# Attention with 16 queries per head: one late store in place of fifteen

## The chip, the cores and the metric

The kernel runs on one core of one Trainium2 chip. Its time is the device time of that core in microseconds (us). The core has a matrix engine (TensorE, PE in the profile), a vector engine (VectorE, DVE), an activation engine (ScalarE, ACT), GpSimd (POOL) and SyncE (SP), which here does nothing but issue transfers. All of them run their own instruction streams and meet at semaphores. Transfers between HBM and SBUF are carried out by 16 DMA engines. SyncE and ScalarE each have a queue to them; in the profile SyncE's is q1 and ScalarE's q10.

## The reference, cut to what matters

```
B, H, Sq, Skv, Dh = 8, 16, 16, 2048, 256        # all bfloat16
scores = einsum('bhqd,bhkd->bhqk', q, k) * Dh ** -0.5
attn   = softmax(scores, axis=-1)
out    = einsum('bhqk,bhkd->bhqd', attn, v)
```

There are 128 heads. K and V are 134 MB each and are read once; q and the output are 1 MB each.

## The kernel before, in words

**Blocks.** Eight heads make a block of 128 rows of output (8 heads by 16 queries); there are G = 16 blocks, numbered 0 to 15, and `last` is 15. A block needs 8 MB of K, which comes as two halves of 4 MB, and 8 MB of V. The 128 rows are the partitions of the result.

**Buffers.** `SL` has four slots of 4 MB in SBUF: VA and VB hold one block's V, KA and KB one block's K. Nothing of K or V is held twice, so a slot is loaded again as soon as its readers are done. `O_fin` holds the finished 128 rows of 256 values of one block in bfloat16, 512 bytes in each partition.

**One block.** VectorE transposes the K slots in place (line 196). TensorE multiplies them with the weights made of q into `S_ps` (lines 309 and 310). VectorE takes the maximum, ScalarE makes the exponentials into `P_sb` with their sums (line 292). VectorE transposes those into `PTa` and `PTb`, and ScalarE and VectorE copy them into `PTz` (lines 277, 203 and 205), the weights of the second product. TensorE sums 128 matmuls of V into `O_ps` (line 332). ScalarE evicts `O_ps` with a factor of one over the sum into `O_fin` (`evac`, line 271), and the block is stored.

**The order around the change.** The engines run loops over the blocks, one block apart from one another. In its pass g ScalarE works on the exponentials of block g, makes the first part of the copies, evicts block g - 1, issues its store, and makes the rest of the copies (lines 284 to 302). The eviction waits for the end of block g - 1's matmuls (`c_pv`), for its factor (`c_ri`) and, since there is only one `O_fin`, for the landing of the store before (`s_st`). The store waits for the eviction (`c_ev`). TensorE starts the next block's second product only when `c_ev` says that `O_ps` is empty.

**SyncE's queue.** SyncE issues every load, in this order: q; K of blocks 0 and 1; V of block 0; then in a loop both K halves of block j and V of block j - 1, each behind a wait for the readers of the slot; then K of block 15 in four pieces, V of block 14 in three pieces, and V of block 15 in nine pieces that get smaller (`PIECES`, the last one of two matmuls' rows). Each V piece waits until the matmuls on the rows that it overwrites are done. Behind the last piece SyncE waits for the last eviction, stores block 15 and waits for its landing:

```
eng.wait_ge(c_ev, G + 1)
eng.dma_start(oh[last], O_fin[:]).then_inc(s_fin, 16)
eng.wait_ge(s_fin, 16)
```

GpSimd gives some semaphores their start values, 1 to `c_ev` and 17 to `s_st` among them, so that the first passes find their waits satisfied.

Of the kernel before, what the change touches and what calls it, by code (L numbers as in the profile page):

```python
# [4 lines left out]
ACTF = mybir.ActivationFunctionType  # L5
# [6 lines left out]
BF16 = mybir.dt.bfloat16  # L12
# [8 lines left out]
def bass_standalone__softmax_full_bidir__sampling_kernel(  # L21
# [6 lines left out]
    B, H, SQ, D = q.shape  # L28
# [3 lines left out]
    G = NH // 8  # L32
    last = G - 1
    scale = float(D) ** -0.5
# [3 lines left out]
    ku = k.rearrange("b h s d -> (b h s) d").rearrange("(u p t) d -> u p t d", p=128, t=T)  # L38
    vb = v.rearrange("b h s d -> (b h s) d").rearrange("(g p t) d -> g p t d", p=128, t=2 * T)
    qh = q.rearrange("b h s d -> (b h) (s d)")  # L40
    oh = out.rearrange("b h s d -> (b h s) d").rearrange("(g p) d -> g p d", p=128)

    with ExitStack() as es:
        ec = es.enter_context
# [8 lines left out]

        PTz = ec(nc.sbuf_tensor("PTz", [128, 2, T, 128], BF16))
        mk = ec(nc.sbuf_tensor("mk", [128, 1], F32))
        O_fin = ec(nc.sbuf_tensor("O_fin", [128, D], BF16))
        negm = ec(nc.sbuf_tensor("negm", [128, 1], F32))
        lsum = ec(nc.sbuf_tensor("lsum", [128, 2], F32))
        ltot = ec(nc.sbuf_tensor("ltot", [128, 1], F32))
        rinv = ec(nc.sbuf_tensor("rinv", [128, G + 2], F32))  # L60

        S_ps = ec(nc.psum_tensor("S_ps", [128, 4, 512], F32))
        O_ps = ec(nc.psum_tensor("O_ps", [128, 512], F32))
        X_ps = ec(nc.psum_tensor("X_ps", [128, 512], F32))

        def sem(name):
            return ec(nc.semaphore(name))
# [4 lines left out]
        s_kl = [sem("s_kla"), sem("s_klb")]  # L72
        s_v = sem("s_v")
        s_v0 = sem("s_v0")
        s_st = sem("s_st")
        s_fin = sem("s_fin")
# [9 lines left out]
        c_ri = sem("c_ri")  # L86
        c_cp = sem("c_cp")
# [3 lines left out]
        c_pv = sem("c_pv")  # L91
        c_ev = sem("c_ev")
# [19 lines left out]
        def weights(e, r, x):  # L112
            rows = slice(32 * r, 32 * r + (32 if x else 16))
            m = 32 * r + 16 * x
            if e == x:
                src = PTa[rows, :, 16 * x:16 * x + 16]
            else:
                src = PTb[rows, e:e + T, 16 * x:16 * x + 16]
            return PTz[rows, e, :, m:m + 16], src, mk[rows, :]

        def qx(Q, a):

            return (QTu[32 * a:32 * a + 32, 8 * Q:8 * Q + 8, :, :].rearrange("p u c y -> p c u y"),
                    QXu[32 * Q:32 * Q + 32, a, :, :, :].rearrange("p u c y -> p c u y"))

        def load_k(eng, g, e, slot, t0, n, s):
            eng.dma_start(SL[:, slot, t0:t0 + n, :], ku[2 * g + e, :, t0:t0 + n, :]).then_inc(s, 16)  # L127

        def on_sync(eng):
            def load_v(w, a, n):  # L130

                eng.wait_ge(c_pv, 8 * w + (a + n + C - 1) // C)
                eng.dma_start(VW[:, a:a + n, :], vb[w, :, a:a + n, :]).then_inc(s_p[w][a] if a else s_v, 16)  # L133

            eng.dma_start(QX, qh).then_inc(s_q, 16)  # L135
            for g, s0, s in ((0, VA, s_k0), (1, KA, s_k)):
                for e in range(2):
                    load_k(eng, g, e, s0 + e, 0, T, s[e])

            for e in range(2):  # L140
                eng.wait_ge(c_qk, 4 * e + 4)
                eng.dma_start(VW[:, T * e:T * e + T, :], vb[0, :, T * e:T * e + T, :]).then_inc(s_v0 if e else s_v, 16)
            with nc.Fori(2, last, engines=[SP]) as j:
                for e in range(2):
                    eng.wait_ge(c_qk, 8 * j + 4 * e - 4)
                    load_k(eng, j, e, KA + e, 0, T, s_k[e])
                load_v(j - 1, 0, 2 * T)
            for e in range(2):
                eng.wait_ge(c_qk, 8 * last + 4 * e - 4)
                load_k(eng, last, e, KA + e, 0, T // 2, s_k[e])  # L150
                load_k(eng, last, e, KA + e, T // 2, T // 2, s_kl[e])
            for w in PIECES:
                for a, n in PIECES[w]:
                    load_v(w, a, n)
            eng.wait_ge(c_ev, G + 1)
            eng.dma_start(oh[last], O_fin[:]).then_inc(s_fin, 16)
            eng.wait_ge(s_fin, 16)

        def on_gpsimd(eng):

            for x, n in ([(c_ev, 1), (c_ri, 2), (c_cp, 1), (c_pv, 8), (s_st, 17)] + [(x, 1) for x in s_kl] +
                         [(x, 1) for w in s_p for x in s_p[w].values()]):
                eng.sem_inc(x, n)
            zero = [PTz[:, e].rearrange("p t c -> p (t c)").bitcast(F32) for e in range(2)]
            eng.memset(zero[0], 0.0).then_inc(c_pool, 1)
            eng.wait_ge(c_qt, 2)
            for n in range(12):

                eng.wait_ge(c_cq if n else c_pool, max(n, 1))
                eng.tensor_copy(*qx(1 + n // 4, n % 4)).then_inc(c_cq, 1)  # L170

            eng.wait_ge(c_qt, 6)
            eng.wait_ge(c_qw, 4)
            eng.wait_ge(c_cq, 12)
            eng.memset(zero[1], 0.0).then_inc(c_pool, 1)
# [81 lines left out]
        def on_scalar(eng):  # L257
            def qwb(src):
                for a in range(4):
                    dv = QW[32 * a:32 * a + 32, :, 16 * a:16 * a + 64, :]  # L260
                    dv = bass.AP(tensor=dv.tensor, offset=QW[32 * a:32 * a + 32, 0, 16 * a, :].offset,
                                 ap=[list(dv.ap[0]), [1024 + 512, 2], [2, 64], [1, 2]])
                    eng.activation(dv, src(a), ACTF.Copy, scale=scale).then_inc(c_qw, 1)  # L263

            def evac(n, st):

                eng.wait_ge(c_pv, 8 * n)
                eng.wait_ge(c_ri, 2 * n)

                eng.wait_ge(s_st, st)  # L270
                eng.activation(O_fin[:], O_ps[:, 0:D], ACTF.Copy, scale=rinv[:, bass.ds(n, 1)]).then_inc(c_ev, 1)  # L271

            def copies(e, rs):
                for r in rs:
                    for x in range(2):
                        dst, src, m = weights(e, r, x)
                        eng.activation(dst, src, ACTF.Copy, scale=m if x else 1.0).then_inc(c_cp, 1)  # L277

            eng.wait_ge(c_qt, 2)
            qwb(lambda a: QXu[0:32, a, 0:2, :, :])  # L280
            eng.wait_ge(c_pool, 2)
            eng.wait_ge(c_qt, 6)
            eng.wait_ge(c_mk, 7)
            with nc.Fori(0, G, engines=[ACT]) as g:
                eng.wait_ge(c_qk, 8 * g + 8)
                qwb(lambda a: QTu[32 * a:32 * a + 32, bass.ds(((g + 1) & 15) * 2, 2), :, :])
                eng.wait_ge(c_mx, g + 1)
                for h in range(2):

                    sv = S_ps[:, 2 * h, :]  # L290
                    sv = bass.AP(tensor=sv.tensor, offset=sv.offset, ap=[list(sv.ap[0]), [32, 32], [1, 2], [2, 16]])
                    eng.activation(P_sb[:, 16 + 1024 * h:16 + 1024 * h + 1024], sv, ACTF.Exp,  # L292
                                   bias=negm[:], scale=1.0, accum_out=lsum[:, h:h + 1]).then_inc(c_ex[h], 1)
                eng.wait_ge(c_pt, 4 * g + 4)
                eng.wait_ge(c_pv, 8 * g + 4)
                copies(0, (0, 1))
                gg = eng.to_reg(g)
                with eng.If_ne(gg, 0):
                    evac(g + 1, 16 * g + 1)
                    eng.wait_ge(c_ev, g + 1)  # L300
                    eng.dma_start(oh[(g + 15) & 15], O_fin[:]).then_inc(s_st, 16)
                copies(1, (0, 1, 2))
            evac(G + 1, 16 * last + 17)

        def on_tensor(eng):
            def mm(dst, w, x, start, stop, load, check=True):
# [47 lines left out]
            with nc.Fori(1, G + 1, engines=[PE]) as r:  # L354
# [20 lines left out]
                pv(lim)  # L375

        on_sync(nc.sync)
        on_gpsimd(nc.gpsimd)
        on_vector(nc.vector)
        on_scalar(nc.scalar)  # L380
        on_tensor(nc.tensor)

# [27 lines left out]
```

## Time and profile before

| what | value |
| --- | --- |
| time, median of 3 runs (lowest to highest) | 634.5 us (634.5 to 634.57) |
| span of the profiled execution, first to last instruction | 633.1 us |
| what the median has over that span | 1.4 us |
| read from HBM, written to HBM | 269.48 MB, 1.05 MB |
| mean rate of the transfers over the span | 427 GB/s |
| mean granted TensorE clock | 0.976 |

The profile is of one execution. A busy time is the time in which an engine runs instructions of its own; instructions that only wait or issue a transfer are not counted. L271 is line 271 of the kernel. In the lists of groups and waits the number behind an arrow is idle time and what ended it. The mean share of the DMA engines is over all 16; a share can come out a little over 1 as the times of packets that follow one another overlap by a few ns. The time to landing of a transfer runs from its issue to its semaphore, so it holds the time that it stood behind others.

### The profile page before, as it was taken

Reading aid. Unit: us, or ns where it says so; the run is one execution under the profiler, and the core shown is the slowest. Engines: PE = TensorE matmul, PEld = TensorE weight load, DVE = VectorE, ACT = ScalarE, POOL = GpSimd, SP = SyncE. Lnnn points to the kernel's source line nnn. Section 1 sums busy time; section 2 is a strip of 40 time slices with the busy share of each in tenths; the row PEclk is TensorE's granted clock in tenths of the full one; section 3 lists DMA queues with packets and bytes.
Section 4 is the critical chain, followed back from the end, with each engine's and each line's share of the span. In section 5 each row is a group of like instructions: output and inputs, shape, how many; then the busy total and the mean of one; then the engine's idle time right before and its main releaser. Section 6 shows DMA issues by size and latency. Waiting matters only on the chain.

```text
span 633.1 us, 8100 instructions
## 1 busy us (share of the span) xinstructions
PE 539.1 (85%) x3336; PEld 273.3 (43%) x2561; DVE 444.2 (70%) x285; ACT 241.8 (38%) x309; POOL 21.5 (3%) x18
## 2 busy tenths in 40 slices
PE   1659989889898897989979899797989979899997
PEld 0112824518244272542725336263362724518386
DVE  5989794865948658496575966759567595769750
ACT  1027542622336233352424425244252442623453
POOL 7600000000000000000000000000000000000000
PEclk9998989999898999989999899999998999999999
DMA  8999999999999999999999999999999999999997
GB/s 366 433 433 437 434 443 424 452 411 441 437 428 436 430 433 461 405 459 406 458 413 425 438 427 437 455 404 460 406 462 409 427 437 429 435 420 428 432 427 297
DMA packets 11234, 270.56 MB, mean 427 GB/s; under 512 B 1248, under 2 KB 3552, under 8 KB 3936
## 3 DMA queue, kind: packets, MB, share of 16 engines
q1 hardware_dynamic: 9072, 269.55, 98.8%
q10 hardware_dynamic: 2160, 0.98, 0.5%
q8 instruction: 1, 0.02, 0.0%
q14 instruction: 1, 0.01, 0.0%
HBM read 269.48 MB, written 1.05 MB: 427 GB/s over the span
## 4 chain that ended last, share of the span: by engine, by line
DMA 57%; PE 32%; DVE 6%; issue 4%; SPq 0%; DVEq 0%; ACT 0%
DMA SL<-in_v_dram 45%; PE O_ps L332 30%; DMA SL<-in_k_dram 12%; DVE SL L196 4%; PE S_ps L309 1%; PE S_ps L310 1%; DVE PTz L203 0%; DVE PTb L231 0%; DVE negm L220 0%; DVE PTz L205 0%; DVE PTa L229 0%; SPq L127 0%; SPq L133 0%; ACT O_fin L271 0%; SPq L135 0%
## 5 line engine op out<-in xcount | busy, mean ns | idle before, releaser
L196 DVE STREAM_TRANSPOSE SL<-SL 128x4096 f32<-128x4096 f32 x64 | 282.3, 4433 | 81.7 <-DMA SL<-in_k_dram 80.8
L309 PE MATMUL S_ps<-SL,QW 128*128 128x512 bf16 (+1 forms) x512 | 206.3, 403 | 68.5 <-DVE SL L196 58.9
L332 PEld LDWEIGHTS O_ps<-SL,PTz 128*128 128x128 bf16 x2048 | 198.8, 98 | 103.0 <-DMA SL<-in_v_dram 79.2
L332 PE MATMUL O_ps<-SL,PTz 128*128 128x256 bf16 x2048 | 226.7, 273 | 13.5 <-DMA SL<-in_v_dram 12.4
L310 PE MATMUL S_ps<-SL,QW 128*128 128x512 bf16 (+1 forms) x512 | 204.8, 400 | 0.0
L309 PEld LDWEIGHTS S_ps<-SL,QW 128*128 128x128 bf16 (+1 forms) x512 | 74.3, 145 | 244.6 <-issue 155.2
L263 ACT ACTIVATE QW<-QT 32x256 bf16 x64 | 26.9, 420 | 202.5 <-PE S_ps L310 201.3
L277 ACT ACTIVATE PTz<-PTa 16x1024 bf16<-16x1024 bf16 x32 | 33.8, 1056 | 112.0 <-PE O_ps L332 100.2
L220 DVE TENSOR_REDUCE negm<-S_ps 128x1 f32<-128x2048 f32 x16 | 36.6, 2289 | 55.1 <-PE S_ps L310 55.1
L310 PE MATMUL X_ps<-QT,QW 128*128 128x512 bf16 x260 | 58.2, 379 | 0.0
L277 ACT ACTIVATE PTz<-PTb 16x1024 bf16<-16x1024 bf16 x48 | 50.6, 1055 | 10.9 <-ACT O_fin L271 10.1
L229 DVE STREAM_TRANSPOSE PTa<-P_sb 128x1024 bf16<-128x1024 bf16 x32 | 39.2, 1224 | 21.9 <-ACT P_sb L292 21.9
L277 ACT ACTIVATE PTz<-PTa,mk 32x1024 bf16<-32x1024 bf16 x48 | 54.3, 1130 | 0.0
L231 DVE STREAM_TRANSPOSE PTb<-P_sb 128x1024 bf16<-128x1024 bf16 (+1 forms) x32 | 39.0, 1218 | 0.0
L292 ACT ACTIVATE P_sb<-S_ps,negm 128x1024 bf16<-128x1024 f32 x32 | 35.4, 1110 | 5.9 <-DVE negm L220 5.9
L277 ACT ACTIVATE PTz<-PTb,mk 32x1024 bf16<-32x1024 bf16 x32 | 36.2, 1132 | 0.0
L271 ACT ACTIVATE O_fin<-O_ps,rinv 128x256 bf16<-128x256 f32 x16 | 7.6, 474 | 51.5 <-PE O_ps L332 51.5
L203 DVE TENSOR_SCALAR PTz<-PTb,mk 32x1024 bf16<-32x1024 bf16 x32 | 15.2, 476 | 0.0
L205 DVE COPY PTz<-PTa 16x1024 bf16<-16x1024 bf16 x32 | 13.5, 422 | 1.6 <-PE O_ps L332 0.6
L170 POOL COPY QT<-PTz 32x1024 bf16<-32x1024 bf16 x12 | 14.3, 1192 | 3.2 <-DVE PTz L187 2.5
L205 DVE COPY PTz<-PTb 16x1024 bf16<-16x1024 bf16 x16 | 6.8, 424 | 3.4 <-PE O_ps L332 3.0
L309 PE MATMUL S_ps<-PTz 128*128 128x512 bf16 x1 | 0.6, 610 | 9.9 <-ACT QW L263 9.9
(21 smaller groups left out, 38.8 us busy)
## 6 DMA issues: line engine op xcount, KB each, us to landing
SL<-in_k_dram SPq DMA_DIRECT2D x30, 4096.0 KB, 24.3
SL<-in_v_dram SPq DMA_DIRECT2D x2, 4096.0 KB, 21.9
SL<-in_k_dram SPq DMA_DIRECT2D x4, 2048.0 KB, 21.1
SL<-in_v_dram SPq DMA_DIRECT2D x2, 2048.0 KB, 18.7
SL<-in_v_dram SPq DMA_DIRECT2D x1, 3584.0 KB, 21.0
SL<-in_v_dram SPq DMA_DIRECT2D x1, 2560.0 KB, 23.6
SL<-in_v_dram SPq DMA_DIRECT2D x1, 1792.0 KB, 11.0
SL<-in_v_dram SPq DMA_DIRECT2D x1, 1472.0 KB, 12.6
```

Of the source, the lines that this page charges most:

```text
L196: eng.transpose(x, x).then_inc(c_kt, 1)
L203: ins = eng.tensor_scalar(out=dst, in0=src, scalar1=m, scalar2=None, op0=ALU.mult)
L205: ins = eng.tensor_copy(dst, src)
L220: eng.tensor_reduce(out=negm[:], in_=S_ps[:].rearrange("p c n -> p (c n)"), axis=AX.X, op=ALU.max, negate=True).then_inc(c_mx, 1)
L229: eng.transpose(fa[:, 1024 * h:1024 * h + 1024], P_sb[:, 16 + 1024 * h:16 + 1024 * h + 1024]).then_inc(c_pt, 1)
L231: eng.transpose(fb[:, 1024 * h:1024 * h + n], P_sb[:, 1024 * h:1024 * h + n]).then_inc(c_pt, 1)
L263: eng.activation(dv, src(a), ACTF.Copy, scale=scale).then_inc(c_qw, 1)
L277: eng.activation(dst, src, ACTF.Copy, scale=m if x else 1.0).then_inc(c_cp, 1)
L292: eng.activation(P_sb[:, 16 + 1024 * h:16 + 1024 * h + 1024], sv, ACTF.Exp, bias=negm[:], scale=1.0, accum_out=lsum[:, h:h + 1]).then_inc( ...
L309: return eng.matmul(dst, w, x, start=start, stop=stop, skip_group_check=not check)
L310: return eng.add_instruction(mybir.InstMatmult(name=nc.get_next_instruction_name(), engine=PE, start_tensor_calc=start, stop_tensor_calc=stop,
L332: ins = eng.matmul(O_ps[:, 0:D], PTz[:, t // T, t % T, :], VW[:, t, :], start=(t == 0), stop=(t == 2 * T - 1))
```

## The change

`O_fin` is replaced by `O_all`, which has room for all blocks: 18 rows of 256 values in each partition, 9,216 bytes in place of 512. The eviction of block b writes row b + 2. ScalarE no longer waits for earlier stores, and in its loop it neither waits for its own eviction nor issues a store. SyncE, behind the issue of the last V piece, waits for the eviction of block 14 and then issues one store of rows 2 to 16, that is blocks 0 to 14: in each of 128 partitions 15 runs of 512 bytes that lie together in SBUF and 64 KB apart in HBM, 0.98 MB in all. Block 15 is stored by ScalarE right behind its eviction. SyncE ends with a wait for both stores. `s_st` is used by the one big store and starts at 0.

```diff
-    oh = out.rearrange("b h s d -> (b h s) d").rearrange("(g p) d -> g p d", p=128)
+    oh = out.rearrange("b h s d -> (b h s) d").rearrange("(g p) d -> p g d", p=128)
...
-        O_fin = ec(nc.sbuf_tensor("O_fin", [128, D], BF16))
+        O_all = ec(nc.sbuf_tensor("O_all", [128, G + 2, D], BF16))
...
         # on_sync
-            eng.wait_ge(c_ev, G + 1)
-            eng.dma_start(oh[last], O_fin[:]).then_inc(s_fin, 16)
+            eng.wait_ge(c_ev, G)
+            eng.dma_start(oh[:, 0:last, :], O_all[:, 2:G + 1, :]).then_inc(s_st, 16)
             eng.wait_ge(s_fin, 16)
+            eng.wait_ge(s_st, 16)
...
         # on_gpsimd
-            for x, n in ([(c_ev, 1), (c_ri, 2), (c_cp, 1), (c_pv, 8), (s_st, 17)] + ...
+            for x, n in ([(c_ev, 1), (c_ri, 2), (c_cp, 1), (c_pv, 8)] + ...
...
         # on_scalar
-            def evac(n, st):
+            def evac(n):
                 eng.wait_ge(c_pv, 8 * n)
                 eng.wait_ge(c_ri, 2 * n)
-                eng.wait_ge(s_st, st)
-                eng.activation(O_fin[:], O_ps[:, 0:D], ACTF.Copy, scale=rinv[:, bass.ds(n, 1)]).then_inc(c_ev, 1)
+                eng.activation(O_all[:, bass.ds(n, 1), :].rearrange("p o d -> p (o d)"), O_ps[:, 0:D], ACTF.Copy,
+                               scale=rinv[:, bass.ds(n, 1)]).then_inc(c_ev, 1)
...
                 with eng.If_ne(gg, 0):
-                    evac(g + 1, 16 * g + 1)
-                    eng.wait_ge(c_ev, g + 1)
-                    eng.dma_start(oh[(g + 15) & 15], O_fin[:]).then_inc(s_st, 16)
+                    evac(g + 1)
                 copies(1, (0, 1, 2))
-            evac(G + 1, 16 * last + 17)
+            evac(G + 1)
+            eng.wait_ge(c_ev, G + 1)
+            eng.dma_start(oh[:, last, :], O_all[:, G + 1, :]).then_inc(s_fin, 16)
```

More of the change, by code (lines that the diff above doesn't have):

```diff
@@ L154, in on_sync @@
                     load_v(w, a, n)
-            eng.wait_ge(c_ev, G + 1)
-            eng.dma_start(oh[last], O_fin[:]).then_inc(s_fin, 16)
+            eng.wait_ge(c_ev, G)
+            eng.dma_start(oh[:, 0:last, :], O_all[:, 2:G + 1, :]).then_inc(s_st, 16)
             eng.wait_ge(s_fin, 16)
+            eng.wait_ge(s_st, 16)
         def on_gpsimd(eng):
-            for x, n in ([(c_ev, 1), (c_ri, 2), (c_cp, 1), (c_pv, 8), (s_st, 17)] + [(x, 1) for x in s_kl] +
+            for x, n in ([(c_ev, 1), (c_ri, 2), (c_cp, 1), (c_pv, 8)] + [(x, 1) for x in s_kl] +
                          [(x, 1) for w in s_p for x in s_p[w].values()]):
```

## The prediction

> **What bounds the kernel now.** I read the page first, then the stretches of the last microseconds, then the waits. The page's DMA row is full from the second slice to the last but one, while no engine is; section 3 gives the two queues that carry everything, q1 (SyncE's) and q10 (ScalarE's, the 15 stores).
>
> ```profile
> span 633.1 us, 8100 instructions
> PE 539.1 (85%) x3336; PEld 273.3 (43%) x2561; DVE 444.2 (70%) x285; ACT 241.8 (38%) x309; POOL 21.5 (3%) x18
> ...
> DMA  8999999999999999999999999999999999999997
> ...
> q1 hardware_dynamic: 9072, 269.55, 98.8%
> q10 hardware_dynamic: 2160, 0.98, 0.5%
> ```
>
> The stretches make it sharp. Their last three columns are the granted clock, the mean busy share of the 16 DMA engines, and GB/s.
>
> ```profile
> core 0: us, PE busy (x) PEld busy (x) DVE busy (x) ACT busy (x) POOL busy (x), PEclk, DMA share, GB/s
> ...
> 50.00:600.00 550.00, 488.01 (x3009) 243.55 (x2270) 395.01 (x250) 219.46 (x276) 0.00 (x0) 0.98 1.00 432
> 600.00:627.00 27.00, 24.68 (x223) 21.30 (x222) 9.61 (x13) 14.91 (x19) 0.00 (x0) 1.00 1.00 421
> 628.20:628.80 0.60, 0.60 (x8) 0.45 (x5) 0.00 (x0) 0.00 (x0) 0.00 (x0) 1.00 0.62 216
> 628.80:629.40 0.60, 0.60 (x7) 0.49 (x6) 0.00 (x0) 0.00 (x0) 0.00 (x0) 1.00 0.15 56
> 629.40:630.10 0.70, 0.70 (x9) 0.62 (x8) 0.00 (x0) 0.00 (x0) 0.00 (x0) 1.00 0.07 23
> 630.10:632.30 2.20, 0.90 (x9) 0.56 (x6) 0.00 (x0) 0.47 (x1) 0.00 (x0) 1.00 0.00 0
> 632.30:632.80 0.50, 0.00 (x0) 0.00 (x0) 0.00 (x0) 0.00 (x0) 0.00 (x0) 1.00 0.44 131
> ```
>
> Until 627 the share is 1.00: the transfers leave no hole. Then the engines finish their loads at different times: 0.60*0.62 + 0.60*0.15 + 0.70*0.07 = 0.51, so the mean one is done at 628.20 + 0.51 = 628.7, while 0.07 of 16 is one engine, and that one works until about 630.0. From 630.1 to 632.3 all sixteen stand still: the last matmuls and the eviction run, and the last store follows. So a kernel bound by its DMA engines ends with about 3 us in which they do nothing but 64 KB.
>
> The compute follows the landings and does not set the pace: in nearly every block VectorE waits for K and TensorE for V, each some 4.7 us (80.8/17, 79.2/17).
>
> ```profile
> DVE SL L196 <- DMA SL<-in_k_dram: 80.8, 17, 6.2
> PEld O_ps L332 <- DMA SL<-in_v_dram: 79.2, 17, 5.9
> ACT PTz L277 <- ACT O_fin L271: 10.1, 15, 0.7
> ...
> PE O_ps L332 <- DVE PTz L203: 1.1, 1, 1.1
> ```
>
> **The change part by part.** 15 stores leave the middle of the stream. What one of them takes of the engines is seen in two places: in the stretch of 24.4 us around one store in the loop (586.4 to 610.8), its queue q10 has 0.9%, that is 0.22 us of all 16 engines; the last store alone, in the 0.50 us row above, has 0.44 of it, again 0.22 us.
>
> ```profile
> DMA packets 723, 10.46 MB, mean 428 GB/s; under 512 B 80, under 2 KB 208, under 8 KB 208
> ...
> q1 hardware_dynamic: 579, 10.39, 99.4%
> q10 hardware_dynamic: 144, 0.07, 0.9%
> ```
>
> As the engines have no idle time before 627, what is taken out of them shortens the stream by as much: 15 * 0.22 = 3.3 us (the page's 0.5% of 633.1 is 3.2, and its rounding bounds it by 2.8 and 3.5). All 15 lie ahead of the last loads, the fifteenth too:
>
> ```profile
> 615.22 0.34 ACTq L301 DMA_DIRECT2D out_dram<-O_fin  x1
> 615.61 1.06 ACT L277 ACTIVATE PTz<-PTb 16x1024 bf16<-16x1024 bf16 x1 [0.67 <-ACT O_fin L271]
> ...
> out_dram<-O_fin ACTq DMA_DIRECT2D x1, 64.0 KB, 12.7
> ```
>
> It lands at 615.22 + 12.7 = 627.9. Without the stores the slowest engine is done with V at 630.0 - 3.3 = 626.7, the mean one at 625.4. The matmuls must follow for that to count. From 615.26 they ran whenever V let them:
>
> ```profile
> 615.26 3.23 PE L332 MATMUL O_ps<-SL,PTz 128*128 128x256 bf16 x28 [1.08 <-DVE PTz L203]
> 619.72 11.28 PE L332 MATMUL O_ps<-SL,PTz 128*128 128x256 bf16 x100 [1.24 <-DMA SL<-in_v_dram]
> ...
> 628.86 1.86 PEld L332 LDWEIGHTS O_ps<-SL,PTz 128*128 128x128 bf16 x18 [0.17 <-DMA SL<-in_v_dram]
> ```
>
> They last waited for V at 628.86, so their end at 619.72 + 11.28 = 631.0 is V's doing and moves to 627.7.
>
> The one big store is added behind the last V piece on SP's queue. Its wait for block 14's eviction delays nothing:
>
> ```profile
> 614.46 0.47 ACT L271 ACTIVATE O_fin<-O_ps,rinv 128x256 bf16<-128x256 f32 x1 [1.57 <-PE O_ps L332]
> ...
> 615.53 0.43 SPq L133 DMA_DIRECT2D SL<-in_v_dram  x1
> ...
> SL<-in_v_dram SPq DMA_DIRECT2D x1, 128.0 KB, 14.9
> ```
>
> That eviction ends at 614.93, the last piece is issued at 615.53 and done issuing at 615.96; behind the wait on SP there is only the store and the end. The piece lands 14.9 us after its issue, so the store is issued at about 616 - 3.3 = 612.7, some 14 us before the slowest engine comes to it. The start of the transfer is hidden by that queue; if that cover were gone it would cost at most the 1.5 us from issue to landing of a whole 64 KB store, below. If making the packets took as long as that for each 64 KB, 15 * 1.5 = 22.5 us, it would stick out by 8; nothing shows 1.5 us being spent on that, so I leave it outside the range.
>
> ```profile
> L301 ACTq DMA_DIRECT2D out_dram<-O_fin x15: 338/338/394, 79.7 to 615.2; - x15
> L156 SPq DMA_DIRECT2D out_dram<-O_fin x1: 344/344/344, 631.5 to 631.5; - x1
> ...
> DMA to landing us min/median/max: 1.5/23.5/23.9
> ```
>
> Its run is the unknown, for no row shows 0.98 MB written in one go. Low end: 15 * 0.22 = 3.3 us, since the bytes and the 512-byte rows are the same and both rows above agree on 0.22. High end: 0.98 MB at the 131 GB/s of the last store's row, 7.5 us. A transfer of nearly its size to an idle queue stands between:
>
> ```profile
> PTz<-in_q_dram SPq DMA_DIRECT2D x1, 1024.0 KB, 5.0
> ```
>
> Those 5.0 us hold a lead of issue and first bytes, which the store pays under cover. I take 3.3, because the 0.50 us stretch also holds the time before the first packet and after the last, so its 131 GB/s is no rate of a running store. On the slowest engine the store then runs from 626.7 to 630.0.
>
> The last block's store goes from SP to ScalarE. SP issued it at 631.54, 0.03 us behind the eviction:
>
> ```profile
> 631.04 0.47 ACT L271 ACTIVATE O_fin<-O_ps,rinv 128x256 bf16<-128x256 f32 x1 [9.11 <-PE O_ps L332]
> ...
> 631.54 0.34 SPq L156 DMA_DIRECT2D out_dram<-O_fin  x1
> ```
>
> ScalarE in the loop needed 0.29 (614.93 to 615.22), which I keep. The eviction ends at 631.51 - 3.3 = 628.2, the store is issued at 628.5 and would land at 630.0 if alone. On the slowest engine its 0.22 us share the line with the big store: 630.0 + 0.2 = 630.2.
>
> Edits in ScalarE's loop: the wait for its own eviction and the issue go, so 0.67 us of idling per block falls to about 0.1 or 0.2. It is worth nothing on the path: ScalarE is busy 38% and the waits list no TensorE wait on its copies in the loop, only 1.1 us on VectorE's. The evicting instruction's wait for the previous store never held, since that lands at most 23.9 us after issue and issues are 39 us apart ((615.2 - 79.7)/14 = 38.7). The destination with the block in its address and GpSimd's dropped start value cost some registers' work under the same cover.
>
> Sum: the last packets at 630.2, plus 0.4 us to the end (the last packets of before lie ahead of 632.8 and the end is at 633.1, so at least 0.3), gives a span of 630.6, which is 2.5 less. The runs' median of 634.5 is 1.4 over the profiled span; with that kept, 632.0.
>
> **The rivals.**
> (a) The big store writes too slowly, and the time is longer. It sits on the end of the path, so each microsecond above 3.3 counts fully: at 3.3 + 2.5 = 5.8 us (0.39 a block) the gain is gone, and at 7.5, the 131 GB/s, the time is 632.0 + 4.2 = 636.2. For it: no row has more than 64 KB of writes together, and each engine's rows now step from block to block, 64 KB apart. Against it: V is read in rows that begin 64 KB apart in HBM at a share of 1.00 and 432 GB/s. The Trainium skill, "DMA: Bandwidth & Descriptors", section "Latency and other measured facts", reports copies whose rows lie a large power of two apart falling from 207 to 103 GB/s, the fall beginning above 512 KiB; at its worst rate the store would take about 9.5 us and the time be about 638 (an estimate from that page), and V's 432 GB/s at 64 KB, though reads, does not show it.
> (b) The store runs as long as the load of Q, 5.0 us: 632.0 + 1.7 = 633.7, no change that can be told. The same page, section "Bandwidth", gives 6.15 us for a load of 1 MB, an estimate of 634.9; the trace's 5.0 us from issue to landing, lead included, is already less.
> (c) Compute does not follow the loads. Then TensorE starts block 15 at 615.26 as now and needs 128 * 0.11 = 14.1 us (11.28/100 each): 629.4 instead of 631.0, 1.6 saved, 632.9. Against it are the two rows of waits for landings.
> (d) The slow engine of the end is not slow in that run, so the big store is wholly covered: the last store alone sets the end, 630.0 + 0.1, and the time is 631.5.
>
> **How the numbers follow.** A measurement of this kernel tells about 0.2% (1.3 us) from no change. Forecast, 632.0 (its own range 631.3 to 633.1, from 2.8 or 3.5 us taken out and a store of up to 4.4 us): 0.58. (d) 0.08 and (c) 0.06 are faster as well: together 0.72. (b), with all stores of about 4.5 to 7 us: 0.12. (a) 0.16, since writing in one go is the one thing unseen. The range from 631.2 to 635.6 leaves out most of (a) and a little below.
>
> **What would show it.** In the profile after: q10 with one store's 144 packets; the share 1.00 up to about 624; matmuls ending near 627.7; the store's packets between about 625 and 630 and then the end, in place of the empty 2.2 us. Wrong would be: stretches at the end with a high share but far fewer GB/s than 64 KB per 0.22 us (a); last V pieces that land no earlier; TensorE late behind VectorE (c); or a gap between the last V packet and the first of the store.

## The result, and the profile after

| | before | after |
| --- | --- | --- |
| time, median | 634.5 us | 632.52 us (632.18 to 632.84, 6 runs) |
| span of the profiled execution | 633.1 us | 631.1 us |
| ratio to the kernel before | | 0.9968, 95% interval 0.9958 to 0.9978 |

The kernel became faster by 2.0 us, 0.32%; the forecast was 2.5. The profiled execution of the changed kernel took 632.44, 1.3 over its span. One of the six runs of the kernel before that were timed beside these took 3,079.66 us, for a reason that nothing here shows, and is left out.

The page of the changed kernel has the transfers full into the last slice, where before the last one stood at 7. Its two queues are here q1 with the big store in it and q10 with the last store alone.

```profile
span 631.1 us, 7943 instructions
...
DMA  8999999999999999999999999999999999999999
...
q1 hardware_dynamic: 10864, 270.47, 99.7%
q10 hardware_dynamic: 144, 0.07, 0.0%
```

The end of the changed kernel in stretches; the last three columns are the granted clock, the share of the DMA engines and GB/s.

```profile
core 0: us, PE busy (x) PEld busy (x) DVE busy (x) ACT busy (x) POOL busy (x), PEclk, DMA share, GB/s
50.00:600.00 550.00, 487.14 (x2962) 245.29 (x2288) 396.62 (x251) 219.15 (x280) 0.00 (x0) 0.97 1.00 432
...
627.30:627.90 0.60, 0.60 (x8) 0.54 (x6) 0.00 (x0) 0.00 (x0) 0.00 (x0) 1.00 1.14 348
627.90:628.80 0.90, 0.86 (x8) 0.52 (x6) 0.00 (x0) 0.00 (x0) 0.00 (x0) 1.00 1.15 348
628.80:630.10 1.30, 0.00 (x0) 0.00 (x0) 0.00 (x0) 0.47 (x1) 0.00 (x0) 1.00 0.47 141
630.10:630.80 0.70, 0.00 (x0) 0.00 (x0) 0.00 (x0) 0.00 (x0) 0.00 (x0) 1.00 0.36 108
630.80:631.10 0.30, 0.00 (x0) 0.00 (x0) 0.00 (x0) 0.00 (x0) 0.00 (x0) 1.00 0.00 0
```

Where the engines stood still while the last matmuls and the eviction ran, they now write. The stretches from 627.3 to 628.8 hold almost nothing but the big store, at 348 GB/s: 512 bytes per engine in 16 * 512 / 348 = 23.5 ns. The packets' records in the trace give such a packet 27 ns; the share of 1.15 is 27/23.5, for each packet's record overlaps the next by some 3.5 ns. The whole store is 0.983 MB / 348 = 2.8 us for each engine.

The instructions of the end, from the timelines of SP, ScalarE, TensorE and its weight loads (PEld), and the list of transfers with their time to landing:

```profile
614.05 0.44 SPq L157 DMA_DIRECT2D out_dram<-O_all  x1
...
628.80 0.47 ACT L271 ACTIVATE O_all<-O_ps,rinv 128x256 bf16<-128x256 f32 x1 [9.65 <-PE O_ps L333]
629.30 0.37 ACTq L304 DMA_DIRECT2D out_dram<-O_all  x1
...
617.58 11.18 PE L333 MATMUL O_ps<-SL,PTz 128*128 128x256 bf16 x100 [1.09 <-DMA SL<-in_v_dram]
...
621.12 7.36 PEld L333 LDWEIGHTS O_ps<-SL,PTz 128*128 128x128 bf16 x68 [0.15 <-DMA SL<-in_v_dram]
...
out_dram<-O_all SPq DMA_DIRECT2D x1, 960.0 KB, 16.9
out_dram<-O_all ACTq DMA_DIRECT2D x1, 64.0 KB, 1.8
```

The matmuls end at 628.8 instead of 631.0, and by the packets' records the last load ends at 627.75 instead of 629.98, so 2.2 us of the stream are gone. The big store lands at 614.05 + 16.9 = 630.95, the last one at 629.30 + 1.8 = 631.1: both arrive together, the last store a little later.

### The profile page after: what moved, and what is told of

Read it like the earlier page. It is cut to its first block, busy times and chain, and to the rows that moved or that the text cites. A ratio compares the mean times of both kernels' runs of the same rounds, so it can differ in the third digit from the quotient of the medians.

```text
span 631.1 us, 7943 instructions
## 1 busy us (share of the span) xinstructions
PE 535.9 (85%) x3271; PEld 273.3 (43%) x2561; DVE 444.2 (70%) x285; ACT 240.0 (38%) x309; POOL 21.5 (3%) x18
## 4 chain that ended last, share of the span: by engine, by line
DMA 56%; PE 36%; DVE 4%; issue 2%; SPq 0%; ACT 0%; DVEq 0%
DMA SL<-in_v_dram 48%; PE O_ps L333 32%; DMA SL<-in_k_dram 8%; DVE SL L198 3%; PE S_ps L310 2%; PE S_ps L311 2%; DVE negm L222 0%; DVE PTz L205 0%; DVE PTz L207 0%; ACT P_sb L293 0%; SPq L134 0%; SPq L128 0%; ACT O_all L271 0%; SPq L136 0%; DVEq L220 0%
## 5 line engine op out<-in xcount | busy, mean ns | idle before, releaser
L311 PE MATMUL X_ps<-QT,QW 128*128 128x512 bf16 x195 | 52.7, 379 | 3.5
L271 ACT ACTIVATE O_all<-O_ps,rinv 128x256 f32 (+1 forms) x16 | 7.6, 474 | 51.4 <-PE O_ps L333 51.4
## 6 DMA issues: line engine op xcount, KB each, us to landing
SL<-in_v_dram SPq DMA_DIRECT2D x1, 2560.0 KB, 23.5
```

Source lines behind the costliest of these rows:

```text
L311: return eng.add_instruction(mybir.InstMatmult(name=nc.get_next_instruction_name(), engine=PE, start_tensor_calc=start, stop_tensor_calc=stop,
```

## The experiments

Three questions were open: whether it is the place of the stores that brings the gain, whether the big store is covered, and why the stream became shorter by 2.2 us and not by 3.3.

**Is it ScalarE's loop?** All 15 stores go back into the loop, from the new buffer and without the wait for the store before.

```diff
                     evac(g + 1)
+                    eng.wait_ge(c_ev, g + 1)
+                    eng.dma_start(oh[:, bass.ds((g + 15) & 15, 1), :], O_all[:, bass.ds(g + 1, 1), :]).then_inc(s_lp, 16)
...
-            eng.wait_ge(c_ev, G)
-            eng.dma_start(oh[:, 0:last, :], O_all[:, 2:G + 1, :]).then_inc(s_st, 16)
```

> The changed kernel, but all 15 stores go out in ScalarE's loop, from the new buffer and without the wait for the store before. Theory (edits in ScalarE's loop are worth nothing): as the kernel before, 634.5 within 0.2. Rival (part of the gain is ScalarE's dropped wait or the buffer): under 634.0.

Measured: 634.59 (634.35 to 634.73), a ratio of 1.0002 (0.9993 to 1.0011). The buffer, the dropped wait and ScalarE's issue of the last store are together worth nothing that can be told; the gain is in moving the 15 stores.

**Is it that fifteen became one?** Blocks 0 to 13 are stored by one transfer ahead of block 15's V pieces, and block 14 alone behind them (its line is left out here).

```diff
             for w in PIECES:
+                if w == last:
+                    eng.wait_ge(c_ev, last)
+                    eng.dma_start(oh[:, 0:last - 1, :], O_all[:, 2:G, :]).then_inc(s_lp, 16)
                 for a, n in PIECES[w]:
                     load_v(w, a, n)
```

> The changed kernel, but the big store has blocks 0 to 13 and SyncE begins it ahead of the pieces of block 15's V; block 14 is stored behind them. Theory (the gain is that the bytes move when the engines would stand still): V ends 14 * 0.19 = 2.6 us later, the span is 630.8 + 2.6 = 633.4, the time 634.7, no better than the kernel before. Rival (one transfer is cheaper than fifteen wherever it is): 632.5.

Measured: 634.81 (634.52 to 635.88), a ratio of 1.0004 (0.9995 to 1.0013). One transfer inside the stream brings nothing; the place at the end is what counts. The profiled execution, 635.88, is the slowest of the eleven: TensorE was granted half its clock just as block 15 began, so the end of its matmuls is not read here. Its loads can be read: by the packets' records the last one ends at 630.5, 2.8 us later than in the changed kernel, where 2.6 was expected.

```profile
615.40:620.00 4.60, 4.51 (x22) 3.21 (x23) 0.00 (x0) 3.77 (x4) 0.00 (x0) 0.50 1.01 430
```

**Half of the stores in the loop.** Blocks 0 to 7 in ScalarE's loop, 8 to 14 in the big store.

```diff
                     evac(g + 1)
+                early = eng.to_reg(((g + 15) & 15) & 8)
+                with eng.If_eq(early, 0):
+                    eng.wait_ge(c_ev, g + 1)
+                    eng.dma_start(oh[:, bass.ds((g + 15) & 15, 1), :], O_all[:, bass.ds(g + 1, 1), :]).then_inc(s_lp, 16)
...
-            eng.dma_start(oh[:, 0:last, :], O_all[:, 2:G + 1, :]).then_inc(s_st, 16)
+            eng.dma_start(oh[:, 8:last, :], O_all[:, 10:G + 1, :]).then_inc(s_st, 16)
```

> The changed kernel, but blocks 0 to 7 are stored in ScalarE's loop as before and the big store has blocks 8 to 14. Theory (a store in the loop lengthens the stream by 0.15 us net): 8 * 0.15 = 1.2 more on the path of the last store, 630.8 + 1.2 = 632.0 span, 633.3. Rival (a store costs its packets' 0.22 us, and the missing 1 us of the forecast went elsewhere): 8 * 0.22 = 1.8, 633.9. Rival (number of stores in the loop does not matter, only that the last one does not wait): 632.5.

Measured: 633.84 (633.7 to 634.02), a ratio of 0.999 (0.9981 to 0.9999), which by itself would speak for the rival's 633.9. The profile speaks for the theory:

```profile
core 0: 632.2 us, clock 0.973
...
630.08 0.47 ACT L273 ACTIVATE O_all<-O_ps,rinv 128x256 bf16<-128x256 f32 x1 [9.69 <-PE O_ps L339]
```

The last eviction comes at 630.08 instead of 628.80, 1.28 later, 0.16 for each of eight stores, and the span is 632.2, where the theory had 632.0 and the rival's 1.8 would give 632.6. Around the span lie 1.6 us in the profiled execution (633.83) instead of 1.3. All eleven runs have 1.6 to 1.7 there, and every run of the other kernels 1.25 to 1.4; why this kernel has 0.3 more stays open.

**Is the big store covered?** It is left out, so that blocks 0 to 14 are not written; the changed kernel ran again on the same chip.

```diff
-            eng.wait_ge(c_ev, G)
-            eng.dma_start(oh[:, 0:last, :], O_all[:, 2:G + 1, :]).then_inc(s_st, 16)
             eng.wait_ge(s_fin, 16)
-            eng.wait_ge(s_st, 16)
```

> The changed kernel without the big store: blocks 0 to 14 are not written. Theory (the big store ends last, on the engine that is last with V, and sticks out a little): the last store alone sets the end, at 630.4 + 0.36 = 630.8 by the changed kernel's trace against 631.1, so about 0.35 us less, 632.2. Rival (the big store is covered whole): no difference, 632.5. Rival (it costs its own 2.8 us): 629.7. The loads should end where they end in the changed kernel, matmuls at 628.8.

> The kernel without the big store once more (blocks 0 to 14 are not written), on the same chip as the changed kernel. Theory (the big store is almost wholly covered): 0.1 to 0.2 us less than the changed kernel. Rival (it sticks out by what the forecast had, the last store's path being 0.5 shorter): 0.5 less.

> The changed kernel once more, beside the others of this group: 632.5 within 0.3, a ratio of 0.997 to the kernel before. If that is wrong, differences of 0.1 or 0.2 us between the experiments are not to be read.

Measured: 632.35 the first time; in the second group 632.33 (632.25 to 632.54) without the store and 632.54 (632.45 to 632.8) with it, the latter 0.9968 (0.9956 to 0.998) of the kernel before. So 0.98 MB of writes stick out by about 0.2 us, less than the 0.35 first expected. That is smaller than the 0.6 us or more to which the intervals of the ratios reach, and rests on both groups of runs agreeing and on the traces. The last store of the kernel without the big one:

```profile
629.35 0.37 ACTq L301 DMA_DIRECT2D out_dram<-O_all  x1
...
out_dram<-O_all ACTq DMA_DIRECT2D x1, 64.0 KB, 1.6
```

Its last store lands 1.6 us after its issue, with the big store beside it 1.8. Without any store of blocks 0 to 14 the end is at nearly the same time: a better place for them has some 0.2 us left to win.

**Does it matter whose queue the last store takes?** SyncE issues it behind the big one.

```diff
             eng.dma_start(oh[:, 0:last, :], O_all[:, 2:G + 1, :]).then_inc(s_st, 16)
+            eng.wait_ge(c_ev, G + 1)
+            eng.dma_start(oh[:, last, :], O_all[:, G + 1, :]).then_inc(s_fin, 16)
...
             evac(G + 1)
-            eng.wait_ge(c_ev, G + 1)
-            eng.dma_start(oh[:, last, :], O_all[:, G + 1, :]).then_inc(s_fin, 16)
```

> The changed kernel, but SyncE issues the last store too, behind the big one on its own queue. Theory (the slowest engine works off both in any order): 632.5, within 0.2 us. Rival (ScalarE's own queue lets the last store pass): 120 packets of 27 ns stand ahead of it on each engine, up to 0.5 us longer, 633.0.

Measured: 632.62 (632.43 to 632.71), 0.997 (0.9958 to 0.9981) of the kernel before. The queue makes no difference that can be told, which fits a slowest engine that has to work off both stores in whatever order.

```profile
out_dram<-O_all SPq DMA_DIRECT2D x1, 960.0 KB, 16.8
out_dram<-O_all SPq DMA_DIRECT2D x1, 64.0 KB, 1.8
```

**Why a store in the loop costs less than its packets.** With saturated engines, the period of a block is the price list. It is read from SP's issues of V, six blocks apart, first in the kernel before, then in the changed one:

```profile
313.05 0.33 SPq L133 DMA_DIRECT2D SL<-in_v_dram  x1
...
546.67 0.33 SPq L133 DMA_DIRECT2D SL<-in_v_dram  x1
```

```profile
312.16 0.33 SPq L134 DMA_DIRECT2D SL<-in_v_dram  x1
...
544.84 0.33 SPq L134 DMA_DIRECT2D SL<-in_v_dram  x1
```

38.94 and 38.78 us: a store in the loop costs 0.16. Its packets take 8 * 23.5 ns and a semaphore write of some 6 ns (9 in the records, less the overlap), 0.19. The records of V's 65,536-byte packets differ with what ran ahead of them on their engine, so I put other small transfers where the store had been, none of use to the result: a copy from SBUF to SBUF, a load of 64 KB of q, and later a copy from HBM to HBM into the rows of block 15, which the last store writes over.

```diff
                     evac(g + 1)
+                    eng.wait_ge(c_ev, g + 1)
+                    eng.wait_ge(s_x, 16 * g + 1)
+                    eng.dma_start(X_sb[:], O_all[:, bass.ds(g + 1, 1), :].rearrange("p o d -> p (o d)")).then_inc(s_x, 16)
# the load:           eng.dma_start(X_sb[:], qh[:, 0:D]).then_inc(s_x, 16)
# HBM to HBM:         eng.dma_start(oh[:, last, :], qh[:, 0:D]).then_inc(s_x, 16)
```

> The changed kernel, with a copy of 64 KB from SBUF to SBUF issued by ScalarE in its loop where the store was (15 copies, no use to the result). In the records, V's 64 KB packets take 2418 ns behind a store's packet and 2422 behind one another. Theory (any small packet between two of V's gives 3.5 ns back): V at 2418, and 15 * 0.15 = 2.3 us more than the changed kernel, 634.8. Rival (it is the write to HBM that helps): V stays at 2422 and the copies cost their whole 15 * 0.19 = 2.9, 635.4.

> The changed kernel, with a load of 64 KB of q (512 bytes in each of 128 rows) issued by ScalarE in its loop where the store was. Theory (any small packet between two of V's gives 3.5 ns back): V at 2418, 634.8. Rival (it is the write to HBM that helps, a read does not): V at 2422, 635.4 or more.

> The changed kernel, with a copy of 64 KB from HBM to HBM issued by ScalarE in its loop where the store was (512-byte rows of q into the rows of block 15, which the last store writes over). Theory (a small transfer's price in the stream goes by its destination: 0.15 us net when it writes HBM, 0.24 when it writes SBUF, from wherever it reads): a block's period 38.93, V's packets at 2418 ns, 632.5 + 15 * 0.15 = 634.8. Rival (reading from SBUF is needed too, so that only a store is cheap): a period of 39.0, V at 2422 or more, 635.9 to 636.2.

Measured: 636.16 (636.03 to 636.24) for the copy, 636.08 (635.91 to 636.31) for the load, 634.77 (634.51 to 634.92) for HBM to HBM, all with the big store at the end. The issues of V in the kernel with the SBUF copy, and in the one with the copy from HBM to HBM:

```profile
313.67 0.33 SPq L136 DMA_DIRECT2D SL<-in_v_dram  x1
...
547.79 0.33 SPq L136 DMA_DIRECT2D SL<-in_v_dram  x1
```

```profile
313.13 0.33 SPq L135 DMA_DIRECT2D SL<-in_v_dram  x1
...
546.73 0.33 SPq L135 DMA_DIRECT2D SL<-in_v_dram  x1
```

Periods of 39.02 and 38.93. Beside the records, each packet being given to the engine whose packet before it ended at that moment (where two engines fit, the choice moves the counts by some ten, not the medians):

```
V packets of 65,536 bytes, by the packet ahead of them      median ns   count   period, us
kernel before: a store's packet                              2418        1423    38.94
changed kernel: another packet of V                          2422        1456    38.78
HBM to HBM copy's packet                                     2418        1438    38.93
SBUF to SBUF copy's packet                                   2424        1450    39.02
load's packet                                                2424        1443    39.02
```

A small transfer that writes HBM costs the stream 0.15 to 0.16 us per 64 KB, one that writes SBUF 0.24, and where it reads makes no difference: copy and load agree, store and HBM copy agree. My first theory, that any small packet gives something back, fell with the copy and the load; the destination decides.

The records also show where the difference lies. The table below is for one engine and one block, against the changed kernel, over the six periods:

```
                                    writes HBM          writes SBUF
the small transfer itself           0.19 us             0.21 us (28.7 ns per packet instead of 27)
V's eight packets                   0.02 shorter        0.02 longer
K's sixteen packets (1217.1 ns)     0.03 shorter        unchanged
together                            0.14                0.23
the period                          0.15 to 0.16        0.24
```

K's packets, then, are shortened as well as V's (1215.5 ns in the mean), although nearly all of them have another packet of K ahead of them in every kernel. So the packet just ahead cannot be the whole reason. What inside the engines does it (that loads and stores share less of their way, say) is not shown.

## Why the prediction was right or wrong, point by point

- **DMA engines as the bound.** Right: the share stays 1.00 to the end of the loads in both kernels, and every edit that put transfers into the stream moved the time.
- **15 stores out of the stream, 3.3 us.** This term was mis-sized: 2.2, by the matmuls' end, and 0.16 * 15 = 2.4 by the period. The 0.2 between these two stays open. I took a store's recorded packet times as its price. They count the overlap of some 3.5 ns twice (0.22 becomes 0.19), and while stores that write HBM run among the loads, V's and K's packets are a little shorter (0.19 becomes 0.14 to 0.16). The packets' records of the kernel before have the same overlap and would have shown it; the shares slightly over 1 could not, since for packets of 1.2 and 2.4 us it is a few thousandths at most.
- **TensorE follows the loads.** Right: its end moved from 631.0 to 628.8, by the same 2.2, and the last hundred matmuls were again begun by V's landing, at 617.58 instead of 619.72. But the last pieces hardly set the end, as I had read it: behind that landing TensorE's weight loads waited once more for V, for 0.15 us, and the hundred matmuls took 11.18 us, 0.11 each. Rival (c) did not come about, since block 15 itself began 2.0 earlier (613.26).
- **The big store behind the loads, 3.3 us, and its lead hidden.** Right in place, 2.8 in size, for the same overlap. It was issued at 614.05, some 13 us before the loads ended, and no gap was seen between them. On the slowest engine it ends at about 627.75 + 2.8 = 630.6, 0.6 later than the sum had it: 1.1 lost on the stream, 0.5 won on the store. Both errors come from the same price of a packet, and that they oppose each other is luck; without it the forecast would have been off by 1.1.
- **The last store.** ScalarE issued it 0.03 us behind the eviction (629.27 to 629.30), not the 0.29 that I kept from the loop. I had put its path 0.5 ahead of the big store. With matmuls 1.1 us later than forecast the two are level: the big store lands at 630.95, and without it the last store lands at 629.35 + 1.6 = 630.95. Together they end at 631.1, the last store last; the step fits its eight packets standing beside the big store's on the slowest engine, as the sum had it (8 * 23.5 ns = 0.19).
- **Edits of ScalarE's loop, nothing.** Right: 634.59 with them and the stores in the loop.
- **The sum.** 630.6 was forecast for the span and 631.1 came; 1.4 was kept around it and 1.3 came.
- **Rivals (a) and (b), a slow store.** Refuted: with rows 64 KB apart in HBM the store ran at 348 GB/s, not 131, nor 5.0 us long. The fall that "DMA: Bandwidth & Descriptors" of the Trainium skill reports for larger powers of two ("Latency and other measured facts") does not show here at 64 KB.
- **Rival (d).** It did not come: its 631.5 is 1.0 below the measured 632.5, and the slow engine was there (in the second run without the big store the share is 0.05 from 627.3 to 627.9, about one engine of sixteen). The big store is nearly covered all the same, because the last store's path is as long.

## What to carry to other kernels

In a kernel whose DMA engines never rest, output can be kept in SBUF and written in the time in which the last loads are being consumed: here 2.8 us of writes cost 0.2. It pays only as far as that idle end reaches, and only at that place: fourteen of the fifteen blocks, written some 20 us earlier (landing at 584.22 + 26.7 = 610.9), brought nothing. Price a transfer in a saturated stream by the change of the loop's period with and without it, not by adding up its packets' recorded times.

## What the runs showed of the hardware that I had not expected

- Among saturated loads, 64 KB in 512-byte rows cost 0.15 to 0.16 us when they are written to HBM and 0.24 when they are written to SBUF, from either source. Most of that step lies in the loads' own packets: V's take 2418.6 ns in the mean beside the former, 2424.5 beside the latter and 2421.6 beside neither.
- Packet records of one engine overlap by some 3.5 ns. For long packets it does not matter; for 512 bytes the recorded 27 ns are 23.5, and the share of the engines reads 1.15.
- From 627.3 to 628.8, with the big store almost alone on the engines, one core wrote 512-byte rows at 348 GB/s.
